# A linear-attention and gated-MLP kernel: key-value state in eight full steps, first loads over two queues, the value splits reordered, the last block halved

## The chip, the cores and the metric

The kernel runs on one core of a Trainium2 chip. Its time is the device time of one execution in microseconds (us); lower is better. A core has five engines with a queue of instructions each: TensorE (PE, with weight loads shown apart as PEld), VectorE (DVE), ScalarE (ACT), GpSimd (POOL) and SyncE (SP), which here only issues DMAs. ScalarE can issue DMAs too. All DMAs are carried out by the core's 16 DMA engines. SBUF is the core's working memory of 128 partitions, PSUM the memory of eight banks into which TensorE writes.

## The reference

The input `x` is 2048 tokens by 640 features, everything in float32. With 32 heads of 20 features each:

```python
xn = _layernorm(x)
qkv = (xn @ wqkv)                          # 640 x 1920
pq, pk = q @ w_phi, k @ w_phi              # per head, 20 x 20
phi_q = concat([softmax(pq), softmax(-pq)])  # 40 features a head
phi_k = concat([softmax(pk), softmax(-pk)])
kv = einsum("bhsf,bhsd->bhfd", phi_k, v)   # per head 40 x 20, summed over tokens
z = phi_k.sum(over tokens)                 # per head 40
o = (phi_q @ kv) / (phi_q @ z + 1e-6)
s = o @ wo
g = silu(gelu(xn @ w1 + b1) @ w2 + b2)     # 640 -> 1536 -> 640
return x + s * g
```

## The kernel before

Tokens are handled in 16 tiles of 128. Every float32 matrix is kept as a high half (a copy rounded to a shorter mantissa) and a low half (what is missing), and a product is three matmuls: high by high, high by low, low by high. A "split" makes these halves: ScalarE copies the high one, and GpSimd or VectorE subtracts it from the original.

The kernel has three phases.

*First phase.* At the start, ten matmuls of constants run on TensorE while the first data arrive. The key projection and the head map `w_phi` are folded into one matrix: `fold_w` multiplies each of five chunks of the transposed key weights (`folds`, loaded from `wqk`) by a block-diagonal matrix `foldb`, which VectorE builds from `w_phi` (`foldc`) and the mask `hmask`; GpSimd makes the mask. The product lies in one of three PSUM banks of kind A, ScalarE takes its high half, VectorE its low half (L183), and then the bank is free. Token tiles are normalised (`norm_a`: statistics, `norm_b` or `norm_act`: scaling), transposed on TensorE (`transpose_x`) and split (`plain`). Then each tile is projected to keys (`project` with `wk`), to values (`value` with `wv`) and later to queries; `feat1` and `feat2` make the exponentials of the feature map, `key_fin` scales them. After every two tiles, `kv_pair` adds them to the key-value state in one PSUM bank, `kvp[0]`: per tile and head one matmul (`kv_acc`) of 32 value columns (20 values, a one, which yields `z`, and columns that belong to the next head) against the head's 40 features. A head's product takes 32 partitions (`32*e`, e from 0 to 3) and 40 columns (`40*s`).

*Second phase.* Twelve units (two token halves by six groups of the hidden layer) compute the MLP: `part` for the first matrix, `down` for the second. Beside it, query features come back from memory, are normalised with `z` (`q_norm`, which needs `z` repeated over all partitions, `zrep`), transposed and written out as `phi_t`. The state is copied out of PSUM in `kv_rest`, its row of `z` is sent to memory and back by `kv_norm` in unit 0, and `kv_state` transposes it and lays it out as the block-diagonal `bdk` and `bdl` in unit 6.

*Third phase.* `num` multiplies `phi_t` by `bdk`; `finish` multiplies by `wo`, by the gate, adds `x` and stores the block of 128 output features by 512 tokens. There are 20 such blocks; the very last one (`end`) is computed in two parts of its columns, each with its own PSUM bank, product, sum and store.

The order on the engines is written by hand in three ways. At the startup all engines run in the order of the code. In the rest of the first phase TensorE and SyncE do, and a scheduler places the work of the others. From the second phase on all engines again run in the order of the code. SyncE issues nearly all loads and stores, in order; a DMA waits until the eighth one before it has landed, since there are eight completion semaphores.

## Time and profile before

| | |
|---|---|
| median of 3 runs | 659.72 us (659.64 to 659.89) |
| profiled execution | 659.86 us, of which the profiled span is 658.1 us |
| TensorE busy | 652.6 us, 99% of the span |
| VectorE, ScalarE, GpSimd busy | 72%, 35%, 58% |
| granted TensorE clock | 0.999 of full speed |
| TensorE waits for other engines behind 1 us | four groups of at most 0.8 us each |
| moved by DMA | 126.97 MB, 193 GB/s on average |

Times in a timeline row are in us from the start of the span; the row gives the start, the time from the first start to the last end, the engine, the line of the kernel, the operation, the tile written and the tiles read, and the number of instructions merged into the row. In square brackets stands the idle time before it and what ended it. A matmul's end is modelled, so that rows of TensorE overlap a little. A row of the chain of waits gives start, length and what the end of the execution then depended on.

### The profile page before, as it was taken

What the parts mean: (1) busy time and instruction counts of PE and PEld (TensorE: products, weight loads), DVE (VectorE), ACT (ScalarE), POOL (GpSimd) and SP (SyncE); (2) the same over time, 40 slices, a digit from 0 to 9 for tenths busy, and PEclk for the clock granted to TensorE, in tenths of its full rate; (3) what the DMA queues carried; (4) which work ended last, traced back from release to release, by engine and by line L of the source; (5) the groups of instructions that cost most, each with busy time, mean ns of one, the idle gap of its engine ahead of it and who ended that gap; (6) DMA issues with size and microseconds to landing.
All of it is one profiled execution on the core that took longest, in us unless ns stands there. A gap on an engine that the chain in (4) does not pass through costs nothing.

```text
span 658.1 us, 11381 instructions
## 1 busy us (share of the span) xinstructions
PE 652.6 (99%) x4437; PEld 568.0 (86%) x4437; DVE 474.1 (72%) x721; ACT 228.3 (35%) x321; POOL 383.7 (58%) x352
## 2 busy tenths in 40 slices
PE   9999999999999999999999999999999999999998
PEld 8999999999999998888888888888888886766867
DVE  5886755888777556768978968759789899853232
ACT  3523313332332227352452454751232424032130
POOL 3655354859577456957778776364462967343321
PEclk9999999999999999999999999999999999999999
DMA  8805162825271226537899799695769499999952
GB/s 319 305 2 148 31 156 86 252 82 157 45 209 66 102 82 231 169 109 251 227 258 316 181 416 333 91 344 218 149 219 234 98 271 205 309 218 253 308 189 81
DMA packets 159678, 126.97 MB, mean 193 GB/s; under 512 B 88976, under 2 KB 127120, under 8 KB 158728
## 3 DMA queue, kind: packets, MB, share of 16 engines
q1 hardware_dynamic: 157320, 115.76, 60.9%
q10 hardware_dynamic: 2304, 10.49, 4.2%
q8 instruction: 35, 0.57, 0.3%
q14 instruction: 19, 0.16, 0.1%
HBM read 81.12 MB, written 45.10 MB: 192 GB/s over the span
## 4 chain that ended last, share of the span: by engine, by line
PE 94%; DMA 3%; DVE 1%; POOL 1%; SPq 0%; issue 0%; DVEq 0%; POOLq 0%
PE pA L331 30%; PE pB L687 24%; PE pB L658 22%; PE pB L842 11%; PE pB L789 2%; PE kv L402 2%; PE pA L172 1%; DMA raw<-in_wv_dram 1%; DMA folds<-in_wqk_dram 1%; DMA xt<-in_x_dram 1%; PE pB L796 1%; POOL wv L147 0%; DMA phi_t<-eq 0%; DVE y L696 0%; POOL e L352 0%
## 5 line engine op out<-in xcount | busy, mean ns | idle before, releaser
L687 PE MATMUL pB<-hs,w2s 128*128 128x512 f32 x720 | 165.7, 389 | 0.0
L687 PEld LDWEIGHTS pB<-hs,w2s 128*128 128x128 f32 x720 | 135.0, 188 | 28.8 <-DVE y L696 0.8
L658 PE MATMUL pB<-xp,w1s 128*128 128x512 f32 x324 | 81.3, 389 | 0.0
L658 PE MATMUL pB<-xd,w1s 128*128 128x512 f32 x324 | 79.3, 389 | 0.0
L357 ACT ACTIVATE e<-e 128x1280 f32<-128x1280 f32 x32 | 40.7, 1273 | 95.5 <-POOL e L352 95.1
L842 PE MATMUL pB<-oT,wo 128*128 128x512 f32 (+2 forms) x315 | 73.0, 383 | 0.0
L658 PEld LDWEIGHTS pB<-xd,w1s 128*128 128x128 f32 x324 | 60.8, 188 | 12.6
L658 PEld LDWEIGHTS pB<-xp,w1s 128*128 128x128 f32 x324 | 60.8, 188 | 12.6
L370 POOL TENSOR_TENSOR eq<-eq,rc 128x1280 f32<-128x1280 f32 x16 | 37.9, 2371 | 56.3 <-DVE rc L746 38.3
L842 PEld LDWEIGHTS pB<-oT,wo 128*128 128x128 f32 x315 | 57.8, 188 | 13.8 <-PE pB L789 2.5
L370 POOL TENSOR_TENSOR e<-e,rc 128x1280 f32<-128x1280 f32 x16 | 39.0, 2441 | 46.4 <-DVE rc L390 46.1
L696 DVE TENSOR_TENSOR y<-pB,y 128x512 f32<-128x512 f32 x100 | 63.2, 676 | 1.4 <-PE pB L687 1.4
L352 POOL TENSOR_TENSOR e<-nr,e 128x640 f32<-128x640 f32 x32 | 44.4, 1388 | 29.2 <-DVE nr L351 24.2
L331 PE MATMUL pA<-wv,xp 128*128 128x320 f32 x384 | 60.0, 310 | 0.3 <-POOL wv L147 0.3
L331 PE MATMUL pA<-wk,xp 128*128 128x320 f32 x384 | 59.7, 310 | 0.0
L663 ACT ACTIVATE pB<-pB,b1t 128x512 f32<-128x512 f32 x48 | 31.8, 662 | 78.7 <-DVE pB L925 28.9
L331 PE MATMUL pA<-wq,xp 128*128 128x320 f32 x384 | 58.8, 309 | 0.0
L331 PEld LDWEIGHTS pA<-wv,xp 128*128 128x128 f32 x384 | 57.0, 188 | 0.5 <-POOL wv L147 0.5
L331 PEld LDWEIGHTS pA<-wk,xp 128*128 128x128 f32 x384 | 56.9, 188 | 0.1
L331 PEld LDWEIGHTS pA<-wq,xp 128*128 128x128 f32 x384 | 56.9, 188 | 0.0
L733 POOL TENSOR_TENSOR ez<-eq,zrep 128x1280 f32<-128x1280 f32 x16 | 47.4, 2960 | 0.9 <-DMA eq<-e_dram 0.9
L430 POOL TENSOR_TENSOR w1s<-raw,w1s 128x640 fp32r<-128x640 f32 (+1 forms) x18 | 27.2, 1513 | 31.4 <-ACT w1s L429 31.3
(138 smaller groups left out, 998.0 us busy)
## 6 DMA issues: line engine op xcount, KB each, us to landing
raw<-in_w_dram SPq DMA_DIRECT2D x42, 320.0 KB, 4.9
e_dram<-e ACTq DMA_DIRECT2D x16, 640.0 KB, 3.6
eq<-e_dram SPq DMA_DIRECT2D x16, 640.0 KB, 5.8
phi_t<-eq SPq DMA_DIRECT2D x64, 160.0 KB, 3.3
phT<-phi_t SPq DMA_DIRECT2D x20, 480.0 KB, 9.5
xt<-in_x_dram SPq DMA_DIRECT2D x16, 320.0 KB, 5.3
xres<-in_xt_dram SPq DMA_DIRECT2D x20, 256.0 KB, 8.5
out_dram<-xres SPq DMA_DIRECT2D x18, 256.0 KB, 5.8
```

Of the source, the lines that this page charges most:

```text
L331: nc.tensor.matmul(ps[:, hf, :HALF], stat_x(q, o, k, a), ws[k][:, b, hf * HALF:(hf + 1) * HALF], start=n == 0, stop=n == 3 * KC - 1)
L352: nc.gpsimd.tensor_tensor(e5[:, :, :, 1, :], nr[:, :, :, None].to_broadcast([P, 2, 16, DH]), e5[:, :, :, 0, :], op=OP.subtract)
L357: nc.scalar.activation(ef, ef, AF.Exp)
L370: nc.gpsimd.tensor_tensor(e3, e3, rc[:, :, None].to_broadcast([P, 64, DH]), op=OP.mult)
L402: nc.tensor.matmul(ps[32 * e:32 * e + 32, 40 * s:40 * s + 40], v[:, 21 * h:21 * h + 32], phi[:, 40 * h:40 * h + 40], start=t == 0 and s == ...
L430: nc.gpsimd.tensor_tensor(sl[:, 1, :n], src, sl[:, 0, :n].bitcast(F32), op=OP.subtract)
L658: nc.tensor.matmul(bank[ch][:], tl[:, a, off + wo_:off + wo_ + P], mov(blk, b), start=new and n == 0, stop=n == len(mms) - 1, skip_group_c ...
L663: nc.scalar.activation(ps, ps, AF.Gelu_apprx_tanh, bias=b1t[:, f:f + 1])
L687: nc.tensor.matmul(ps[:], ws[i][:, b, d * P:(d + 1) * P], hs[o][i][:, a, :], start=i == n == 0, stop=(i, n) == (GF - 1, 2), skip_group_che ...
L696: nc.vector.tensor_tensor(y, ps[:], y, op=OP.add)
L733: nc.gpsimd.tensor_tensor(zv, ef, zf, op=OP.mult)
L842: nc.tensor.matmul(ps[:, mv], w, o[:, mv], start=n == 0, stop=n == 15, skip_group_check=True)
```

## The change

Five things are changed together.

1. `kv_acc` places the heads anew. Six steps of four heads stay as they are; the last eight heads, which took three steps of three, three and two, take two steps of four. The state's columns go from 360 to 320. `kv_rest` copies the state to SBUF without the fills, with columns 240 to 320 twice; `kv_state` makes four transposes instead of three and five products for `bdk` instead of one; `kv_norm` sends eight small rows instead of five.
2. The first loads: of the five chunks of key weights, the first and the fourth go out on ScalarE's queue, and token tile 0 between them; the others stay with SyncE.
3. At the startup, `norm_a(0)` comes ahead of the first fold and `norm_b(0)` behind it, and `split_v(1)` comes ahead of `norm_act(2)`.
4. The head mask is made by two GpSimd instructions over six columns instead of twelve over one, and ahead of the identity.
5. The last block's parts are 256 and 256 columns instead of 384 and 128.

```diff
+    nc.gpsimd.memset(hmask, 1.0)
+    nc.gpsimd.affine_select(out=hmask, in_=hmask, pattern=[[-DH, 6]], compare_op=OP.is_ge, fill=0.0, base=0,
+                            channel_multiplier=1)
+    nc.gpsimd.affine_select(out=hmask, in_=hmask, pattern=[[DH, 6]], compare_op=OP.is_ge, fill=0.0, base=DH - 1,
+                            channel_multiplier=-1)
     ident = const.tile([P, P], F32, name="ident")
...
-    for k in range(6):
-        nc.gpsimd.affine_select(out=hmask[:, k:k + 1], in_=hmask[:, k:k + 1], pattern=[[0, 1]],
-                                compare_op=OP.is_ge, fill=0.0, base=-DH * k, channel_multiplier=1)
...
-    def load_fold(which, mid=None):
+    def load_fold(which, engs):
         tl = folds[:, which]
-        for c in range(KC):
-            nc.sync.dma_start(tl[:, c], wqk[which, c, :, :6 * P].rearrange("p (i t) -> p i t", i=6))
-            if c == 1 and mid is not None:
-                mid()
+        for c, eng in enumerate(engs):
+            if c == 1 and which:
+                x_in(0, nc.scalar)
+            eng.dma_start(tl[:, c], wqk[which, c, :, :6 * P].rearrange("p (i t) -> p i t", i=6))
...
     def kv_acc(t, phi, v):
         ps = kvp[0]
-        for g in range(3):
-            for r in range(3):
-                for e in range(4):
-                    h = 3 * (4 * g + e) + r
-                    if 4 * g + e < NFT and h < H:
-                        s = 3 * g + r
-                        nc.tensor.matmul(ps[32 * e:32 * e + 32, 40 * s:40 * s + 40], v[:, 21 * h:21 * h + 32],
-                                         phi[:, 40 * h:40 * h + 40], start=t == 0 and s == 0, stop=t == NT - 1,
-                                         skip_group_check=True)
+        for s in range(8):
+            for e in range(4):
+                h = 3 * (4 * (s // 3) + e) + s % 3 if s < 6 else 24 + 2 * e + s - 6
+                nc.tensor.matmul(ps[32 * e:32 * e + 32, 40 * s:40 * s + 40], v[:, 21 * h:21 * h + 32],
+                                 phi[:, 40 * h:40 * h + 40], start=t == 0 and s == 0, stop=t == NT - 1,
+                                 skip_group_check=True)
...
-    wkT = load_fold(1, lambda: x_in(0))
+    wkT = load_fold(1, (nc.scalar, nc.sync, nc.sync, nc.scalar, nc.sync))
...
+    norm_a(0)
     fold_w(wkT, range(1), "wk", wk_s)
-    norm_a(0)
-    fold_w(wkT, range(1, 2), "wk", wk_s)
     norm_b(0)
-    fold_w(wkT, range(2, 4), "wk", wk_s)
+    fold_w(wkT, range(1, 4), "wk", wk_s)
...
+    split_v(1)
     norm_act(2)
-    split_v(1)
     split_v(2)
...
-        kvr = const.tile([P, 360], F32, name="kvr")
-        nc.gpsimd.memset(kvr[64:96, 320:360], 0.0)
-        nc.gpsimd.memset(kvr[96:, 240:360], 0.0)
-        for p, a, b in ((P, 0, 240), (96, 240, 320), (64, 320, 360)):
-            nc.scalar.activation(kvr[:p, a:b], kvp[0][:p, a:b], AF.Copy)
+        kvr = const.tile([P, 424], F32, name="kvr")
+        nc.scalar.activation(kvr[:, :320], kvp[0][:, :320], AF.Copy)
+        nc.scalar.activation(kvr[:, 320:400], kvp[0][:, 240:320], AF.Copy)
...
-        for g, m in enumerate((P, P, 96)):
-            nc.tensor.transpose(ps[:120, g * P:g * P + m], kvr[:m, 120 * g:120 * g + 120], ident[:m, :m])
...
+        for i, o in enumerate((0, 120, 240, 280)):
+            nc.tensor.transpose(ps[:120, i * P:(i + 1) * P], kvr[:, o:o + 120], ident[:])
+
+        def heads_of(f, n, blk, h, m):
+            src = ps[:120, 32 * blk:32 * (blk + n)].rearrange("p (f r) -> p f r", r=32)
+            nc.vector.tensor_tensor(bdk[:120, f:f + n, 20 * h:20 * (h + m)].rearrange("p f (h d) -> p f h d", d=20),
+                                    src[:, :, None, :20].to_broadcast([120, n, m, 20]),
+                                    mask[:120, None, h:h + m, None].to_broadcast([120, n, m, 20]), op=OP.mult)
+
+        heads_of(0, 8, 0, 0, 3)
+        heads_of(8, 1, 8, 0, 2)
+        heads_of(8, 1, 9, 2, 1)
+        heads_of(9, 1, 13, 0, 1)
+        heads_of(9, 1, 14, 1, 2)
...
-        for e, m in enumerate((3, 3, 2, 2)):
-            nc.sync.dma_start(zv[e:e + 1, :m], kvr[32 * e + 20:32 * e + 21, :120 * m].rearrange("p (g r) -> p g r", r=120))
-        nc.sync.dma_start(z_dram[1200:2 * D].unsqueeze(0), kvr[84:85, 240:320])
+        for e in range(4):
+            one = kvr[32 * e + 20:32 * e + 21]
+            nc.sync.dma_start(zv[e:e + 1], one[:, :240].rearrange("p (g r) -> p g r", r=120))
+            nc.sync.dma_start(zl[e:e + 1], one[:, 240:320])
...
-        parts = (slice(0, 384), slice(384, 512)) if end else (slice(0, W2), slice(W2, 512))
+        parts = (slice(0, W2), slice(W2, 512))
```

The orders on the engines below are those of the built kernels; a number behind a name tells one buffer from another. First VectorE at the startup, before; `wk0` to `wk2` are the folded key weights, whose low halves these products are, and `xt_153` is token tile 0.

```order
L489 TENSOR_TENSOR folds_74<-folds_74 120x6x120
L183 TENSOR_TENSOR wk0_197<-pA_190,wk0_197 128x640
L196 BN_STATS st_200<-xt_153 128x6 x2
L197 BN_AGGR st_200<-st_200 128x2
L198 TENSOR_SCALAR st_200<-st_200 128x1
L183 TENSOR_TENSOR wk1_213<-pA_206,wk1_213 128x640
L212 TENSOR_SCALAR xt_153<-xt_153,st_200 128x640
L183 TENSOR_TENSOR wk2_224<-pA_217,wk2_224 128x640
```

The same place in the changed kernel, where token tile 0 is `xt_142`:

```order
L482 TENSOR_TENSOR folds_74<-folds_74 120x6x120
L195 BN_STATS st_180<-xt_142 128x6 x2
L196 BN_AGGR st_180<-st_180 128x2
L197 TENSOR_SCALAR st_180<-st_180 128x1
L182 TENSOR_TENSOR wk0_193<-pA_186,wk0_193 128x640
L211 TENSOR_SCALAR xt_142<-xt_142,st_180 128x640
L182 TENSOR_TENSOR wk1_204<-pA_197,wk1_204 128x640
L182 TENSOR_TENSOR wk2_214<-pA_207,wk2_214 128x640
```

The statistics of tile 0 have moved ahead of the first low half, and its normalising ahead of the second.

ScalarE at the startup, before: the normalising of tiles 1 and 2 (`xt_158`, `xt_160`), the high halves of the value weights (`wv`, from `raw`) and of token tile 1 (`b12`, `xp`).

```order
L218 ACTIVATE xt_158<-xt_158,st_245 128x640 [waits DMAHW7_49,DVE_49]
L145 ACTIVATE wv_269<-raw_162 128x640 [waits DMAHW1_49]
L251 ACTIVATE b12_304<-pA_298 128x2x128 [waits PE_49]
L251 ACTIVATE xp_73<-pA_298 128x3x128
L218 ACTIVATE xt_160<-xt_160,st_263 128x640 [waits DMAHW0_49,DVE_49]
L145 ACTIVATE wv_317<-raw_164 128x640 [waits DMAHW2_49]
L145 ACTIVATE wv_320<-raw_166 128x640 [waits DMAHW3_49]
```

The same engine now, from its second instruction on and, behind the line of dots, at the same place as above (tiles 1 and 2 are `xt_148` and `xt_150`):

```order
L163 DMA folds_74<-in_wqk_dram 128x768
L139 DMA xt_142<-in_x_dram 128x640
L163 DMA folds_74<-in_wqk_dram 128x768
L181 ACT_TABLE_LOAD
...
L144 ACTIVATE wv_259<-raw_152 128x640 [waits DMAHW1_49]
L250 ACTIVATE b12_294<-pA_288 128x2x128 [waits PE_49]
L250 ACTIVATE xp_73<-pA_288 128x3x128
L144 ACTIVATE wv_305<-raw_154 128x640 [waits DMAHW2_49]
L217 ACTIVATE xt_150<-xt_150,st_253 128x640 [waits DMAHW0_49,DVE_49]
L144 ACTIVATE wv_310<-raw_156 128x640 [waits DMAHW3_49]
```

Three DMAs now stand ahead of the load of the activation table, and the second value split ahead of the normalising of tile 2.

TensorE at the end of the kernel, before, and behind the line of dots now; a block is 15 matmuls with `wo` and one with the last heads' part `wol`:

```order
L842 MATMUL pB<-oT,wo 128x384 x15
L842 MATMUL pB<-oTl,wol 128x384
L842 MATMUL pB<-oT,wo 128x128 x15
L842 MATMUL pB<-oTl,wol 128x128
...
L843 MATMUL pB<-oT,wo 128x256 x15
L843 MATMUL pB<-oTl,wol 128x256
L843 MATMUL pB<-oT,wo 128x256 x15
L843 MATMUL pB<-oTl,wol 128x256
```

The number of instructions is the same; their columns are 256 in both parts.

More of the change, by code (lines that the diff above doesn't have):

```diff
@@ L135, in hedgehog_gated_mlp_kernel, with load_x @@
     bdl = const.tile([P, 120], F32, name="bdl")
-    def load_x(t):
+    def load_x(t, eng=None):
         xt = row([P, D], F32, "xt")
-        nc.sync.dma_start(xt[:], x[_tok(t) * P:(_tok(t) + 1) * P, :])
+        (eng or nc.sync).dma_start(xt[:], x[_tok(t) * P:(_tok(t) + 1) * P, :])
         return xt
@@ L456, in load_w2, with x_in @@
         return [load_split(w2[f * P:(f + 1) * P, :], "w2s", None, lo) for f in range(g * GF, (g + 1) * GF)]
-    def x_in(t):
-        xts[t] = load_x(t)
-    def fold_loads(which, mid=None):
-        return load_fold(which, mid)
+    def x_in(t, eng=None):
+        xts[t] = load_x(t, eng)
     phase1 = ExitStack()
@@ L478, in hedgehog_gated_mlp_kernel @@
         x_in(t)
-    wqT = load_fold(0)
+    wqT = load_fold(0, (nc.sync,) * KC)
     x_in(6)
@@ L632, in kv_norm @@
     def kv_norm(kvr):
[L633 to L636 removed]
+        zv = z_dram[:960].rearrange("(g e r) -> e g r", e=4, r=120)
+        zl = z_dram[960:2 * D].rearrange("(e r) -> e r", e=4)
+        for e in range(4):
+            one = kvr[32 * e + 20:32 * e + 21]
+            nc.sync.dma_start(zv[e:e + 1], one[:, :240].rearrange("p (g r) -> p g r", r=120))
+            nc.sync.dma_start(zl[e:e + 1], one[:, 240:320])
```

10 lines of the change are left out of this document (1 added, 9 removed).

## The prediction

> **What bounds the kernel now.** I read the page first, then TensorE's waits, then the timeline of the places that the diff touches.
>
> ```profile
> PE 652.6 (99%) x4437; PEld 568.0 (86%) x4437; DVE 474.1 (72%) x721; ACT 228.3 (35%) x321; POOL 383.7 (58%) x352
> PE 94%; DMA 3%; DVE 1%; POOL 1%; SPq 0%; issue 0%; DVEq 0%; POOLq 0%
> ```
>
> TensorE is busy nearly always, and 94% of the chain that ended last is its own work. Of its waits for others behind the warm-up, all below a microsecond, two lie in the first 28 us:
>
> ```profile
> PE pA L172 <- DMA folds<-in_wqk_dram: 0.8, 1, 0.8
> ...
> PE pA L331 <- POOL wv L147: 0.3, 1, 0.3
> ```
>
> So a saving on any other engine is worth a fraction of a microsecond at most. What pays is TensorE time taken away, or the first 28 us, where TensorE still waits for its inputs. The profiled execution took 659.86 us around a span of 658.1, against a median of 659.72: 0.14 is to be taken off at the end. The measurement can tell about 0.2%, or 1.3 us, from no change.
>
> **The change: the key-value state in eight full steps.** Each of the 16 token tiles accumulates 32 heads by matmuls of 32 output columns, side by side on four column groups. Before, a tile took nine steps of 4,4,4,4,4,4,3,3,2 heads; now it takes eight of 4. The number of matmuls stays at 32 a tile. The first rows are the last of eight pairs of tiles on TensorE and the projection behind it; the others count the matmul records of that pair that began by the end of each stretch (us from the span's start).
>
> ```profile
> 241.79 1.48 PE L402 MATMUL kv<-e,v 128*32 128x40 f32 x128
> ...
> 243.20 2.03 PE L331 MATMUL pA<-wq,b 128*128 128x320 f32 x12
> ```
> ```profile
> 241.75:241.88 0.12, 0.09 (x8) 1.00 0.00 0
> 241.75:242.13 0.38, 0.34 (x36) 1.00 0.00 0
> ...
> 241.75:242.88 1.13, 1.09 (x111) 1.00 0.00 0
> ```
>
> A pair has 64 matmuls but 128 records, two a matmul. Among the full steps, from 241.88 to 242.13, 28 records start in 0.25 us: 9 ns each, so a step of four matmuls (8 records) takes 72 ns. At that pace 121 would have begun by 242.88, 1.09 us after the first; there are 111, so steps of three and two heads pass fewer matmuls in the same time. 18 steps of 72 ns make 1.30 us and leave 0.11 for running in and out of the 1.41 from 241.79 to 243.20. So I read the pace as per step, whatever it holds. Sixteen steps make 1.15 + 0.11 = 1.26. Eight pairs save 8 x 0.144 = **1.15 us**, on an engine that doesn't wait between 28 and 550 us; so it reaches the end. Its bounds are nothing, if the pace were by the number, and 1.15.
>
> **First loads over two queues, and the new order behind them.** The scalar engine's queue now issues the first weight chunk, token tile 0 and the fourth chunk; the sync queue has the rest. The rows are from the timeline and, the one of DMA xt, from the chain.
>
> ```profile
> 0.84 4.36 PE L469 MATMUL pA<-const-float32-1.0 128*128 128x128 f32 x20 [0.84 <-PEq L1090]
> 1.26 0.90 SPq L162 DMA_DIRECT2D folds<-in_wqk_dram  x2
> ...
> 7.31 0.82 DVE L183 TENSOR_TENSOR wk<-pA,wk 128x640 fp32r<-128x640 f32 x1 [2.60 <-ACT wk L182]
> 8.05 0.88 DVE L196 BATCH_NORM_STATS2 st<-xt 128x6 f32<-128x320 f32 x2
> ...
> 8.67 2.91 PE L172 MATMUL pA<-folds 120*128 120x120 f32 x24 [0.79 <-DMA folds<-in_wqk_dram]
> ...
> 9.28 0.81 DVE L183 TENSOR_TENSOR wk<-pA,wk 128x640 fp32r<-128x640 f32 x1
> 10.04 0.61 DVE L212 TENSOR_SCALAR xt<-xt,st 128x640 f32<-128x640 f32 x1
> 11.01 0.82 DVE L183 TENSOR_TENSOR wk<-pA,wk 128x640 fp32r<-128x640 f32 x1 [0.35 <-ACT wk L182]
> 11.96 1.53 PE L172 MATMUL pA<-folds 120*128 120x120 f32 x12
> ...
> 13.32 3.83 PE L331 MATMUL pA<-wk,xp 128*128 128x320 f32 x24
> ```
> ```profile
> 2.20 5.39 DMA xt<-in_x_dram
> ```
>
> Token tile 0 lands at 7.59 and the third chunk at about 8.6, where the third fold stops waiting. The fifth fold at 11.96 takes over the PSUM bank of the third, which DVE gives up at 11.83; the first projection follows at 13.32. The four mask instructions that now come first on GpSimd make the fold's right-hand side ready earlier; that is worth nothing, since TensorE's warm-up takes it to 5.2 anyway.
>
> How much earlier the loads land is unknown. Lower end: not at all. Then DVE, which now takes the statistics of tile 0 ahead of the first low half (3 instructions, 8.05 to 9.28, so 1.23), runs from 7.6: statistics to 8.9, low half 9.7, normalising 10.3, second low half 11.1, third 11.9. The fifth fold would start at 12.0: nothing won. Upper end: each load by its earlier issue. An issue takes 0.45 (two in 0.90), so tile 0, second on its queue, goes out at about 1.25 instead of 2.20, and the third chunk, third on the other queue, at 1.7 instead of 2.65; landing 0.95 earlier, tile 0 comes at 6.65. The first high half is there at 7.3 and the statistics end at 7.9; third low half 11.0, projection 12.4: 0.9 won. Between them the DMA engines' own slack decides:
>
> ```profile
> 5.00:6.00 1.00, 1.00 (x11) 1.00 (x11) 0.00 (x0) 0.00 (x0) 0.20 (x2) 1.00 0.70 221
> ...
> 9.00:10.00 1.00, 1.00 (x12) 1.00 (x11) 0.97 (x3) 0.00 (x0) 0.56 (x1) 1.00 1.03 410
> ```
>
> From 5 to 6 us they were 70% busy (the column before the last); by 9 they are full. What earlier issue can fill is some 0.3 us, nearest to the lower end; I take **0.3** earlier. The sync queue's later loads move up by three issues, with none of them waited for in time. The activation table load moves behind three issues of 0.45, from 0.8 to 2.2, and ScalarE's first work comes after 6.5: nothing.
>
> **Value splits.** The second split moves ahead of the normalising of tile 2 on ScalarE.
>
> ```profile
> 19.67 0.92 ACT L218 ACTIVATE xt<-xt,st 128x640 f32<-128x640 f32 x1 [1.08 <-DVE st L217]
> ...
> 21.30 3.11 POOL L147 TENSOR_TENSOR wv<-raw,wv 128x640 fp32r<-128x640 f32 x2 [1.82 <-DMA folds<-in_wqk_dram]
> ...
> 23.56 3.98 PE L331 MATMUL pA<-wv,xp 128*128 128x320 f32 x26
> ...
> 26.18 1.57 POOL L147 TENSOR_TENSOR wv<-raw,wv 128x640 fp32r<-128x640 f32 x1
> ...
> 27.81 0.85 PE L331 MATMUL pA<-wv,xp 128*128 128x320 f32 x4 [0.27 <-POOL wv L147]
> ```
> ```profile
> 31.84 8.80 PE pA L331 x60
> ```
>
> The last row is from the chain: 147 ns a projection matmul of 320 columns. The high half of split 1 (0.7, as the ScalarE copies of that size) fits into the 1.08 in which ScalarE sat idle before 19.67. GpSimd then starts its low half at 19.5 instead of 21.30; split 2 follows at 21.3 and the last, still behind the exponent's differences, ends near 26.5 instead of 27.75. TensorE needed it at 27.4 (26 matmuls of 147 ns after 23.56) and got on at 27.81: **0.4** saved, or nothing if the loads make the rest late.
>
> **Last block in halves.** Rows of TensorE, of DVE behind it, and of the output stores.
>
> ```profile
> 650.23 2.79 PE L842 MATMUL pB<-oT,wo 128*128 128x384 f32 x15
> ...
> 653.03 1.79 PE L842 MATMUL pB<-oT,wo 128*128 128x128 f32 x15
> ...
> 654.66 0.28 PE L842 MATMUL pB<-oTl,wol 120*128 120x128 f32 x1
> ```
> ```profile
> 651.35 0.42 DVE L844 TENSOR_TENSOR y<-pB,y 128x256 f32<-128x256 f32 x1
> ...
> 654.97 0.29 DVE L844 TENSOR_TENSOR y<-pB,y 128x128 f32<-128x128 f32 x1 [0.52 <-PE pB L842]
> ```
> ```profile
> out_dram<-xres SPq DMA_DIRECT2D x2, 128.0 KB, 1.9
> ```
>
> Sixteen matmuls of 384 columns take 2.80, 175 ns each; those of 128 columns 109 each (15 from 653.03 to 654.66), twice what their columns would take on the same line, so a floor. 256 columns aren't in the trace: the straight line from 320 (147) through 384 gives 120, the mean between 109 and 175 gives 142. I take 120, since the floor lies below it. The last one then starts at 650.23 + 31 x 0.12 = 653.95 instead of 654.66: 0.7 saved. DVE's two instructions at the end take 0.42 for 0.29, +0.3; the store carries 64 KB more, +0.2 at the 410 GB/s seen above. That nets 0.2; I take **0.1**, since 256 columns may lie a little above the line. With 142 it is 0.5 lost.
>
> **The state's use.** One transpose more on TensorE (three cost 0.24, from 420.46 to 420.70): **0.1** lost.
>
> ```profile
> 420.46 0.47 PE L623 MATMUL pB<-ident,kvr 128*120 128x128 f32 x3
> 420.70 1.64 PE L687 MATMUL pB<-hs,w2s 128*128 128x512 f32 x6
> ```
> ```profile
> 424.03 0.39 DVE L629 TENSOR_TENSOR bdl<-pB,mask 80x40 f32<-80x40 f32 x3
> ...
> 427.82 0.69 DVE L694 COPY y<-pB 128x512 f32<-128x512 f32 x1 [0.67 <-PE pB L687]
> ```
> ```profile
> 249.01 2.78 SPq L635 DMA_DIRECT2D z_dram<-kvr  x4
> ...
> 274.33 2.96 POOL L733 TENSOR_TENSOR ez<-eq,zrep 128x1280 f32<-128x1280 f32 x1
> ```
>
> DVE gets four small products more, 0.13 each like the three here; its idle 0.67 soon after covers them, and if it didn't, the copies out of PSUM would be late. The sync queue sends eight rows of the normaliser instead of five, 0.7 each, so the replicated copy and the loads behind it go out about 2 us later, with 18 us before their first reader. ScalarE copies the state in two pieces instead of three, and GpSimd loses two fills; neither is waited for.
>
> Sum: -1.15 - 0.3 - 0.4 - 0.1 + 0.1 = -1.85. The profiled 659.86 becomes 658.0, the median 657.9.
>
> **Rivals.** *Loads land as before.* The DMA share of 1.0 at 9 us speaks for it, the 0.70 against. Then the 0.3 is gone: 658.2. [...]
>
> *The two queues alternate finely.* Then the second chunk lands with tile 0 and the third with the fourth, at 7.6 and about 9.5 (384 KB a chunk, 0.95 at 410 GB/s): the third fold starts 0.9 later and so does the projection. Sum -0.65 (-1.85 + 0.3 + 0.9): 659.1, no measurable change. Nothing in the trace of before has two queues at once.
>
> *The state is paced by its matmuls.* Then 1.15 is gone: 659.0. The cumulative counts speak against it. [...]
>
> *Slower: tile 0 is late.* DVE now stands before its first low half until tile 0 has landed, and every low half, fold and projection queue behind it. Up to 7.6 this costs nothing; from there each microsecond delays the first projection by one. The other terms save 1.5, so it decides from 9.2, and measurably from 10.5. If the sync queue's chunks are served first, tile 0 lands like the fifth chunk, at about 10.5 (8.6 plus two of 0.95): 2.9 later, 661.1. Its place second on a queue of its own speaks against it.
>
> **How the numbers follow.** Forecast 0.48; loads as before 0.18; fine alternation 0.14; paced by number 0.10; tile 0 late 0.10. The forecast's own range is 657.2 to 658.4, by 0 to 0.9 at the start and 0.5 at the tail. The range 657.0 to 659.3 takes in the next three and leaves out the late tile and the tails. Faster by over 0.2% means under 658.4: most of the first two cases, 0.63. Same: the rest of these, the third and fourth, 0.27. Slower 0.10.
>
> **What would show it.** From the start of a state pair to the next projection: 1.26, not 1.41. The first projection at about 13.0. TensorE waits for no value split. Last matmuls at 0.12 each, the last store out 0.3 earlier than at 655.6. Wrong would be: a pair of 1.41, a first fold or statistics that wait for tile 0 beyond 8 us, or a new wait on TensorE between 250 and 275 or after 424 us.

## The result, and the profile after

The changed kernel takes 658.55 us (median of 13 runs, 658.04 to 658.90) against 659.89 (13 runs, 659.49 to 660.50): a ratio of 0.9978, with a 95% interval of 0.9970 to 0.9987. That is 1.3 us faster (0.9 to 2.0). The forecast was 1.85 faster, 657.9, with a range of 657.0 to 659.3. The profiled execution took 658.55 with a span of 656.8, so 1.31 less than the one of before.

First the busy times of the page after, and what is left of TensorE's waits:

```profile
PE 651.7 (99%) x4438; PEld 567.1 (86%) x4438; DVE 472.9 (72%) x725; ACT 228.5 (35%) x320; POOL 381.3 (58%) x340
```
```profile
PE pA L462 <- PEq L1091: 0.8, 1, 0.8
PE pB L797 <- DVE y L697: 0.4, 1, 0.4
```

The waits for the third weight chunk (0.8) and for the value split (0.3) are gone; the bound is the same. Now the timeline of the kernel after, at the places to which the prediction gave a term (start, us, engine, line, operation):

```profile
5.24 6.05 PE L171 MATMUL pA<-folds 120*128 120x120 f32 x48
6.00 0.89 DVE L195 BATCH_NORM_STATS2 st<-xt 128x6 f32<-128x320 f32 x2 [1.35 <-DMA xt<-in_x_dram]
...
13.03 1.20 PE L330 MATMUL pA<-wk,xp 128*128 128x320 f32 x6
...
23.29 4.56 PE L330 MATMUL pA<-wv,xp 128*128 128x320 f32 x30
24.47 1.57 POOL L146 TENSOR_TENSOR wv<-raw,wv 128x640 fp32r<-128x640 f32 x1
27.68 1.92 PE L330 MATMUL pA<-wv,b 128*128 128x320 f32 x12
...
240.26 1.37 PE L398 MATMUL kv<-e,v 128*32 128x40 f32 x128
241.57 2.02 PE L330 MATMUL pA<-wq,b 128*128 128x320 f32 x12
...
419.01 0.60 PE L613 MATMUL pB<-ident,kvr 128*120 128x128 f32 x4
419.36 3.02 PE L688 MATMUL pB<-hs,w2s 128*128 128x512 f32 x12
...
648.92 1.97 PE L843 MATMUL pB<-oT,wo 128*128 128x256 f32 x15
...
652.65 0.28 PE L843 MATMUL pB<-oTl,wol 120*128 120x256 f32 x1
652.96 0.42 DVE L845 TENSOR_TENSOR y<-pB,y 128x256 f32<-128x256 f32 x1 [0.96 <-PE pB L843]
```

Going by the starts of the same matmuls in the two traces, the kernel after is 0.29 us ahead at the first projection (13.03 for 13.32) and 0.81 ahead at the second value projection (27.68 for 28.49), so the split gave 0.52. From the first matmul of a pair to the next projection it took 1.41 in all eight pairs before; now it takes 1.30 in two of them (the last, from 240.26 on, is one) and 1.32 in the six others, which makes 0.77. With what the projections just behind the pairs gain, the lead grows by 0.83, to 1.64 at 246 us. From there it shrinks: 0.19 in the first feed-forward unit, 0.13 from the transposes on; 1.31 are left at 648.92, against 650.23. In the last block matmuls of 256 columns follow each other at 0.12 and the last one starts 2.0 earlier than before. From the block's start to the landing of the last store (655.78 by its semaphore, 657.25 before) it takes 6.86 instead of 7.02, so 0.16 are won; the closing behind the landing takes 0.17 longer and eats it.

That longer closing is no accident of one execution. From the last landing to the end of the span it takes 0.90 in all four profiles of kernels with the old state, and 1.06 to 1.09 in all ten with the new one. Behind its wait for the last store SyncE still checks one other semaphore in the former and four in the latter, 0.06 each. The state's eight rows instead of five make three transfers more in all (346 for 343), and the last store then has another semaphore, whose turn in these checks comes earlier.

The place in the first feed-forward unit was not in the prediction. Before and after, on DVE, GpSimd and TensorE:

```profile
252.74 2.64 DVE L147 TENSOR_TENSOR w2s<-raw,w2s 128x640 fp32r<-128x640 f32 x2 [2.44 <-ACT w2s L145]
252.93 1.76 POOL L352 TENSOR_TENSOR e<-nr,e 128x640 f32<-128x640 f32 x1
254.66 1.32 POOL L418 TENSOR_TENSOR st<-raw 128x256 f32<-128x256 f32 x1
256.06 0.74 POOL L418 TENSOR_TENSOR st<-st,raw 128x256 f32<-128x256 f32 x1
257.94 2.20 PE L658 MATMUL pB<-xp,w1s 128*128 128x512 f32 x9
```
```profile
250.88 1.27 POOL L351 TENSOR_TENSOR e<-nr,e 128x640 f32<-128x640 f32 x1
251.16 2.94 DVE L146 TENSOR_TENSOR w2s<-raw,w2s 128x640 fp32r<-128x640 f32 x2 [2.44 <-ACT w2s L144]
252.11 1.32 POOL L414 TENSOR_TENSOR st<-raw 128x256 f32<-128x256 f32 x1
253.51 1.20 POOL L414 TENSOR_TENSOR st<-st,raw 128x256 f32<-128x256 f32 x1
256.35 2.33 PE L659 MATMUL pB<-xp,w1s 128*128 128x512 f32 x9
```

Without the two fills GpSimd begins its exponent differences (`e`) before DVE begins to split two weight tiles, and not behind. In the trace, whichever of the two begins second is the slower one: before, DVE's first split takes 0.83 and GpSimd's differences 1.76; now the differences take 1.27 and DVE's first split 1.67. The second split takes 1.90 before and 1.36 now, so the two splits together take 2.94 instead of 2.64. TensorE's nine matmuls behind take 2.33 instead of 2.20; with 0.06 just ahead of them, that is the 0.19.

### The profile page after: what moved, and what is told of

It is laid out like the page before. It is cut to its first block, busy times and chain, and to the rows that moved or that the text cites. A ratio compares the mean times of both kernels' runs of the same rounds, so it can differ in the third digit from the quotient of the medians.

```text
span 656.8 us, 11378 instructions
## 1 busy us (share of the span) xinstructions
PE 651.7 (99%) x4438; PEld 567.1 (86%) x4438; DVE 472.9 (72%) x725; ACT 228.5 (35%) x320; POOL 381.3 (58%) x340
## 4 chain that ended last, share of the span: by engine, by line
PE 98%; DVE 1%; DMA 0%; SPq 0%; issue 0%; DVEq 0%
PE pA L330 32%; PE pB L688 24%; PE pB L659 22%; PE pB L843 11%; PE pA L171 2%; PE pB L790 2%; PE kv L398 2%; PE pA L462 1%; PE pB L797 1%; PE pA L316 1%; DVE y L697 0%; DMA phi_t<-eq 0%; DVE wolh L767 0%; DVE dn L364 0%; SPq L756 0%; DVE wol L768 0%
## 5 line engine op out<-in xcount | busy, mean ns | idle before, releaser
L843 PE MATMUL pB<-oT,wo 128*128 128x512 f32 (+1 forms) x315 | 72.3, 381 | 0.0
L659 PEld LDWEIGHTS pB<-xp,w1s 128*128 128x128 f32 x324 | 60.7, 188 | 12.8 <-DVE pB L926 0.3
```

What stands on the lines that cost most here:

```text
L659: nc.tensor.matmul(bank[ch][:], tl[:, a, off + wo_:off + wo_ + P], mov(blk, b), start=new and n == 0, stop=n == len(mms) - 1, skip_group_c ...
L843: nc.tensor.matmul(ps[:, mv], w, o[:, mv], start=n == 0, stop=n == 15, skip_group_check=True)
```

## The experiments

Times are compared with runs of the kernel before on the same chip. A few tenths can't be told from the medians, so terms are read from the traces and the medians are given beside them.

**Each part alone.** The state alone:

```diff
-        for g in range(3):
-            for r in range(3):
...
+        for s in range(8):
+            for e in range(4):
+                h = 3 * (4 * (s // 3) + e) + s % 3 if s < 6 else 24 + 2 * e + s - 6
...
-        kvr = const.tile([P, 360], F32, name="kvr")
+        kvr = const.tile([P, 424], F32, name="kvr")
```

> The kernel before with the key-value state in eight full steps, and with the state's copy, transposes, products and normaliser rows that belong to it; nothing else. Theory S (the prediction's): a state pair is paced by its steps alone, 72 ns each, so the pair goes from 1.41 to 1.26 us and the kernel loses 1.15 us, less 0.1 for the fourth transpose: about 1.05. Theory P (read from the kernel after, where the pair took 1.30 to 1.32): a step of two or three heads cost about half a full one, so the pair goes to 1.30 to 1.32, eight pairs give 0.8 and, with the transpose, some 0.7 remains. Theory N (paced by the number of matmuls): nothing, the pair stays at 1.41. The small stall of TensorE in the first feed-forward unit of the kernel after (0.15 to 0.2) comes here too if it stems from the state's new order, and stays away if it stems from the earlier start of that unit by more than this edit gives.

Measured: 659.82 against 659.91, ratio 1.0002 (0.9993 to 1.0011): nothing. The same kernel once more, to see whether that holds:

> The kernel with the state alone once more, without any other edit, for a second profile and more times: its first ones were 0.1 us faster than the kernel before, where the pairs alone save 0.7 to 0.8. Theory T: the wait near 139 us goes with the round trip near 78 us; a trip below 4.3 leaves TensorE without a wait there and the end 0.4 earlier than the kernel before, a trip of 4.6 or more brings the wait back. Rival (the wait belongs to this edit whatever the trip): the wait is there at any trip.

Measured: 659.86 against 659.74, ratio 1.0002 (0.9993 to 1.0011). The pairs do take 1.30 to 1.32 in both profiles (one of them 1.36), as theory P has it, but the gain is given back. In the second profile TensorE's lead over the kernel before grows by 0.42 in the four pairs up to 131 us, loses 0.65 at a value projection near 139, gains 0.42 in the other four pairs, loses 0.21 in the first feed-forward unit and 0.15 from the transposes on. The closing, 0.16 longer, takes more. The place near 139, and one on ScalarE ahead of it, of this kernel:

```profile
105.07 0.33 ACTq L384 DMA_DIRECT2D e_dram<-e  x1
105.81 0.74 ACT L251 ACTIVATE xp<-xr 128x640 fp32r<-128x640 f32 x1 [0.77 <-ACT e L357]
...
139.60 0.18 DVE L351 TENSOR_TENSOR nr<-mn,mx 128x32 f32<-128x32 f32 x1
139.82 1.99 PE L331 MATMUL pA<-wv,b 128*128 128x320 f32 x12 [0.42 <-DVE nr L351]
```

and of the kernel before:

```profile
105.06 0.33 ACTq L384 DMA_DIRECT2D e_dram<-e  x1
105.49 0.74 ACT L251 ACTIVATE xp<-xr 128x640 fp32r<-128x640 f32 x1 [0.46 <-ACT e L357]
...
139.25 0.18 DVE L351 TENSOR_TENSOR nr<-mn,mx 128x32 f32<-128x32 f32 x1
140.06 1.19 PE L331 MATMUL pA<-wv,b 128*128 128x320 f32 x7
```

TensorE starts 0.22 behind DVE's difference `nr` when it waits for it, and 0.81 behind when it doesn't, so the kernel before had a margin of 0.6 there. And ScalarE starts its copy 0.41 after the DMA issue ahead of it instead of 0.10, in all profiles with the state alone and in none of the others, the kernel after among them. What holds it there isn't settled. So undoing the other parts wasn't a clean cut: it added a stall of its own.

The loads alone, and the value splits alone:

```diff
-    wkT = load_fold(1, lambda: x_in(0))
+    wkT = load_fold(1, (nc.scalar, nc.sync, nc.sync, nc.scalar, nc.sync))
```

> The kernel before with the first loads over two queues, the mask first and the statistics of tile 0 ahead of the first low half; state, value splits and last block as before. In the kernel after, TensorE's matmuls of the warm-up and the first folds changed from 213 to 112 ns apart at 6.35 us; in the kernel before at 4.81. Theory C (what the loads give is decided by the moment of that change): the folds follow each other without a wait from 5.2, and the first projection starts near 12.4 if the change comes at 4.8, near 13.0 if it comes at 6.35, half a microsecond per microsecond of delay while folds are running. Theory L (the prediction's: the loads land only 0.3 earlier): 13.0 whatever the moment of the change, with a wait for a load left in the folds.

```diff
-    norm_act(2)
     split_v(1)
+    norm_act(2)
```

> The kernel before with the second value split moved ahead of the normalising of tile 2; nothing else. The prediction's theory: TensorE's wait of 0.27 us for the fourth value split disappears and the second value projection starts 0.4 earlier than 28.49, so about 28.1, and the end comes 0.4 earlier. Rival: the wait in the kernel before was set by the splits behind the second one (their weights or GpSimd's exponent differences), and the wait stays or only half of it goes: 28.3 to 28.5.

The loads give 659.52, ratio 0.9995 (0.9987 to 1.0004); the splits 659.38, ratio 0.9992 (0.9983 to 1.0001), both against 659.91. With the loads alone the first projection starts at 12.80 and no fold waits, and the wait for the split is still there. That is nearer to theory C (the change from 213 to 112 ns comes at 5.9 here) than to theory L, since no fold waits for a load. With the splits alone the wait for the split is gone:

```profile
5.24 5.82 PE L171 MATMUL pA<-folds 120*128 120x120 f32 x48
...
12.80 3.84 PE L330 MATMUL pA<-wk,xp 128*128 128x320 f32 x24
...
27.29 0.85 PE L330 MATMUL pA<-wv,xp 128*128 128x320 f32 x4 [0.27 <-POOL wv L146]
```
```profile
23.24 4.56 PE L331 MATMUL pA<-wv,xp 128*128 128x320 f32 x30
27.64 1.92 PE L331 MATMUL pA<-wv,b 128*128 128x320 f32 x12
```

From the first value matmul to the next projection it took 4.93 before (23.56 to 28.49), and takes 4.40 now, so 0.53. The prediction's theory holds, its 0.4 counted the wait and not the gap of 0.1 that restarting costs.

The last block in halves alone:

```diff
-        parts = (slice(0, 384), slice(384, 512)) if end else (slice(0, W2), slice(W2, 512))
+        parts = (slice(0, W2), slice(W2, 512))
```

> The kernel before with the last block in two halves of 256 columns instead of 384 and 128; nothing else. The prediction's theory: the last matmul starts 0.7 earlier, DVE's last two instructions and the bigger last store give back 0.6, so 0.1 is won. Rival, read from the kernel after: the store takes 0.28 and DVE 0.26 longer and the rest is lost in the last wait, so nothing is won or lost: within 0.1 of the kernel before from the start of the last block (650.23) to the last landing (657.25), which is 7.02 us there.

Measured: 659.71 against 659.91, ratio 0.9997 (0.9989 to 1.0006). In the trace, from the block's start (649.97) to the last landing (656.84) 6.87 instead of 7.02: 0.15, near the 0.1 of the prediction, and the rival that nothing is won falls. The medians of the four parts alone add up to 1.0 to 1.2 us (0.1 or -0.1, 0.4, 0.5, 0.2); the whole gives 1.3.

**What a step costs.**

```diff
-        for s in range(8):
+        for s in range(9):
...
-                h = 3 * (4 * (s // 3) + e) + s % 3 if s < 6 else 24 + 2 * e + s - 6
+                h = 3 * (4 * (s // 3) + e) + s % 3 if s < 6 else 24 + 2 * e + (s - 6) % 2
```

> The kernel after with a ninth step of four heads added to the state; the step repeats heads of the seventh, its sums land in columns that nothing reads, so this kernel does work that isn't needed. The pair took 1.30 to 1.32 us after and 1.41 before. Theory S (the prediction's: every step costs 72 ns whatever it holds, and 0.11 is for running in and out): nine steps are nine steps, the pair takes 1.41 again and the time is that of the kernel before less the other parts. Theory F (a full step is 72 ns, running in and out is 0.15, so the three short steps before cost 0.066 each, nearly but not quite a full one: 1.41 less 12 full steps of 0.072 and less 0.15, divided by 6): the pair takes 1.45 to 1.47. Theory N (by the number of matmuls): 1.30 x 72 / 64 = 1.47 as well, but N would have left the pair at 1.41 in the kernel after, which it did not.

Measured: 659.30 against 659.88, 0.75 slower than the kernel after. From the chain of waits, the last pair with nine full steps, and with eight (after):

```profile
241.04 1.45 PE kv L398 x142
```
```profile
240.33 1.30 PE kv L398 x126
```

One full step more in each tile costs about 0.145 a pair (1.448 to 1.468 for 1.303 to 1.323, and one pair of 1.481): 72 ns a step, theory F. Nine steps with three short ones took 1.41; theory S, under which they would be the same, falls. Theory N, by the number of matmuls, gives the same 1.47 here; it falls because the same 64 matmuls went from 1.41 to 1.30. A short step cost 0.066 in the mean, which is what is left of 1.41 when the 12 full steps take 72 ns each and running in and out 0.15; so theory P's half of a full step falls too. Eight pairs at 0.145 make 1.16, but the medians differ by 0.75: in the profile the first projection starts at 12.58 here, 0.45 earlier than in the kernel after, and that hides the rest.

**The second queue.**

```diff
-    wkT = load_fold(1, (nc.scalar, nc.sync, nc.sync, nc.scalar, nc.sync))
+    wkT = load_fold(1, (nc.sync,) * KC)
...
-                x_in(0, nc.scalar)
+                x_in(0)
```

> The kernel after with all first loads on the sync queue, tile 0 again behind the second chunk; mask, statistics and the rest as after. Theory Q (the second queue is what brings the loads earlier): the landings go back to about those of before (tile 0 7.6, third chunk 8.5), the statistics wait until 7.6 and hold back the first low half, TensorE waits for the folds again, and the first projection starts at 13.3 or a little later. Theory M (the mask first and the order of DVE do it, or the loads come earlier by chance): 13.0 or earlier, with tile 0 near 6.0. The moment at which the spacing of the matmuls goes from 213 to 112 ns is to be taken off: up to 0.4 us of start for a change at 4.2 instead of 6.35, as far as the folds are running by then.

Measured: 658.79 against 659.88, 0.24 slower than the kernel after by medians. Timeline:

```profile
7.34 0.89 DVE L195 BATCH_NORM_STATS2 st<-xt 128x6 f32<-128x320 f32 x2 [3.46 <-DMA xt<-in_x_dram]
8.84 2.91 PE L171 MATMUL pA<-folds 120*128 120x120 f32 x24 [1.12 <-DMA folds<-in_wqk_dram]
13.49 2.81 PE L330 MATMUL pA<-wk,xp 128*128 128x320 f32 x17
```

Tile 0 is back at 7.3, the third fold waits 1.1, the projection starts at 13.49. Theory Q: the second queue is what brings the loads (with tile 0's place in it, which this edit moves too). What it does to the rate, from the stretches of before and of after (the last two columns are the share of the DMA engines and GB/s):

```profile
3.00:4.00 1.00, 1.00 (x7) 1.00 (x7) 0.20 (x1) 0.00 (x0) 1.00 (x9) 1.00 1.08 353
4.00:5.00 1.00, 1.00 (x7) 1.00 (x7) 0.70 (x1) 0.00 (x0) 1.00 (x3) 1.00 1.03 287
```
```profile
3.00:4.00 1.00, 1.00 (x7) 1.00 (x7) 0.26 (x1) 0.49 (x1) 0.13 (x1) 1.00 1.04 412
4.00:5.00 1.00, 1.00 (x6) 1.00 (x6) 0.65 (x1) 0.00 (x0) 0.00 (x0) 1.00 1.04 402
5.00:6.00 1.00, 1.00 (x7) 1.00 (x6) 0.01 (x1) 0.00 (x0) 0.00 (x0) 1.00 1.05 415
```

From 3 to 6 us it moves 412, 402 and 415 GB/s where one queue moved 353, 287 and 221 in the kernel before, and 341, 362 and 281 in this run. The second queue brings more than the time of issuing: tile 0 is issued 0.94 earlier with two queues than in this run (1.25 for 2.19), but lands 1.35 earlier (5.97 for 7.32). Why one queue moves less isn't settled. Its issues, 0.45 each, come faster than the chunks land (0.95 apart from 7.6 to 10.4 us in the kernel before), and the DMA engines of the kernel before were counted 30% idle only from 5 to 6 us; from 3 to 5 they were counted full (1.08 and 1.03 in the rows above) while they moved less.

**The warm-up.**

```diff
-        for i in range(5):
+        for i in range(4):
             nc.tensor.matmul(pw[:, 0, :P], one, one, start=True, stop=True)
```

> The kernel after with eight instead of ten warm-up matmuls on constants. In the kernel after the folds follow the warm-up without a wait, from 5.24, and the right-hand side of the folds is ready at 4.65. Theory W (TensorE's own work sets the start now): the folds start at about 4.7 and the first projection up to half a microsecond earlier than 13.03; exactly 0.85 less work at 213 ns or 0.44 at 112 ns, cut by a wait for the right-hand side or the first chunk. Rival (fewer matmuls ahead make the change from 213 to 112 ns come later, and the folds pay for it): the change comes after 6.35, and the first projection starts at 13.0 or later.

Measured: 658.35 (658.07 to 658.51) against 659.88; against the 658.55 of the kernel after no difference that can be told. Timeline:

```profile
4.88 2.94 PE L171 MATMUL pA<-folds 120*128 120x120 f32 x24 [0.48 <-DVE folds L482]
8.36 2.91 PE L171 MATMUL pA<-folds 120*128 120x120 f32 x24 [0.55 <-DMA folds<-in_wqk_dram]
13.02 3.25 PE L330 MATMUL pA<-wk,xp 128*128 128x320 f32 x20
```

The folds start 0.4 earlier, wait 0.55 for the third chunk, and the projection starts where it did. Neither theory quite holds: the change from 213 to 112 ns came early (4.1), against the rival, but the time saved at the front was lost to a load that came at 8.3 in this execution.

Over all profiles, the start goes by two things. One is the moment at which TensorE's matmuls go from 213 to 112 ns apart; the trace's record of the granted clock begins at that moment (the table of stretches shows 1.00 all through), at 4.8 us in the kernel before, at 6.35 in the kernel after, and at 4.1 to 6.5 over all profiles. With two queues and no wait of a fold for a load of over 0.12 us the first projection starts at 12.58 for a moment of 5.0, at 12.64 for 5.5, at 12.80 for 5.9 and at 13.03 for 6.35; in two profiles a fold came 0.2 to 0.3 late, and it starts at 12.60 for 4.6 and at 12.95 for 5.5. What sets that moment, which lies 2.4 us apart in the earliest and the latest profile, isn't shown. The other is the queues: these six profiles with two queues have a mean of 12.8, six with one queue as before start the projection at 12.99 to 13.61 (mean 13.2). So the edits at the start are worth 0.4 in the mean; the two single profiles of before and after happened to show 0.29.

**The unit with the two fills.**

```diff
-        kvr = const.tile([P, 424], F32, name="kvr")
+        kvr = const.tile([P, 584], F32, name="kvr")
+        nc.gpsimd.memset(kvr[64:96, 424:464], 0.0)
+        nc.gpsimd.memset(kvr[96:, 464:584], 0.0)
```

> The kernel after with two fills on GpSimd put back, of the size of those that the change removed and at their old place (they write columns that nothing reads, so they are work that isn't needed). In the first feed-forward unit the kernel after and the one with the state alone gave back 0.15 us of TensorE time, the kernels with the loads, the splits or the halves alone did not. Theory G (the two fills of 0.12 and 0.19 us held GpSimd's exponent differences back until DVE's split of two weight tiles was nearly over; without them GpSimd's work lies beside that split, which takes 2.94 instead of 2.64, and the exchange of DVE against GpSimd makes TensorE wait): the split takes 2.64 again, TensorE waits for no copy there, and 0.15 us come back although GpSimd does more. Rival (the wait comes from the eight normaliser rows on the sync queue, or from the shorter copies on ScalarE): the split stays at about 2.9 and the wait stays.

```profile
250.75 2.64 DVE L146 TENSOR_TENSOR w2s<-raw,w2s 128x640 fp32r<-128x640 f32 x2 [2.44 <-ACT w2s L144]
255.87 2.20 PE L661 MATMUL pB<-xp,w1s 128*128 128x512 f32 x9
```

Theory G: the split takes 2.64 again, the nine matmuls 2.20, and TensorE's lead over the kernel after grows by 0.19 at this place. The median is 658.44, no difference that can be told from 658.55, and three of the ten runs took 659.8 to 660.9, where the kernel after never took more than 658.9. So the 0.19 is shown in the trace alone; that the whole kernel gains by the fills is not shown. The same on the kernel with the state alone:

> The kernel before with the state in eight full steps and the two fills on GpSimd left in at their old place (into columns that nothing reads). With the state alone the gain of 0.7 to 0.8 us in the pairs was given back at three places: 0.40 at the value projection near 139 us, 0.16 in the first feed-forward unit, 0.14 at the four transposes. Theory G: the 0.16 does not come. Theory T: what is given back near 139 depends on how long the statistics' round trip near 78 us happens to take in this execution: nothing below 4.3, up to 0.4 at 4.7. Then the end lies 0.2 to 0.6 before the kernel before. Rival (the state's steps save nothing at the end, whatever the execution): the same time as the kernel before, with TensorE waiting at the same two places.

Measured: 659.48 against 659.74 by medians, 0.38 below the state alone; but three of the eleven runs took 661.3 to 662.3, so that the ratio is 1.0006 (0.9996 to 1.0017) and nothing is won that can be told. Why kernels with the fills have such long runs isn't known. In the trace nothing is lost in the unit; 0.15 is lost near 139 and 0.10 at the transposes. The gap on ScalarE is 0.41 here too. The round trip's own length (4.66, 4.44 and 4.69 us in the three profiles with the state) doesn't order the losses near 139 (0.42, 0.65, 0.15), so theory T falls in the form in which it was put; TensorE's lead on arriving there does (0.55, 0.82, 0.29), against a difference that comes at 139.60 to 139.64 in all three.

**The place near 139 us.** Times from the traces (us): DVE's statistics of token tile 10, whose load comes behind a round trip of statistics through DRAM; the difference `nr`; the value projection.

| kernel | statistics | `nr` | from one to the other | projection behind `nr` |
|---|---|---|---|---|
| before | 88.93 | 139.25 | 50.32 | 0.81 |
| state alone, first and second | 89.08, 89.04 | 139.64, 139.60 | 50.56, 50.56 | 0.22, 0.22 |
| loads alone | 89.06 | 139.32 | 50.26 | 0.22 |
| splits alone | 88.65 | 138.97 | 50.32 | 0.24 |
| after | 87.79 | 138.01 | 50.22 | 0.82 |
| after, with fills | 87.87 | 138.10 | 50.23 | 0.30 |
| after, eight warm-up matmuls | 88.30 | 138.51 | 50.21 | 0.29 |

Whatever TensorE does, `nr` comes 50.2 to 50.3 behind the statistics (50.6 with the gap on ScalarE): a second bound runs through DVE, GpSimd and ScalarE beside TensorE, and TensorE is 0 to 0.6 behind it. The other profiles up to here fit: 50.2 to 50.3 with the halves alone, one queue or nine steps, 50.5 with the state and the fills, which has the gap on ScalarE. With nine steps TensorE comes 1.15 behind `nr`, and `nr` comes no later for it. To make it later, two small reads that nothing uses went ahead of the broadcast read:

```diff
+            if q == 4:
+                for i in range(2):
+                    idle = const.tile([P, 2], F32, name=f"idle{i}")
+                    nc.sync.dma_start(idle[:], st_dram[q, i])
```

> The kernel after with two small reads of the statistics' DRAM copy put ahead of the broadcast read of the second pair of tiles (near 78 us), on the sync queue; nothing reads what they bring, so they only make that round trip longer. In the profiles so far the round trip there (from the store's issue to the broadcast read's) took 3.92 to 4.67 us, and the time between DVE's last difference of the following pair and the value projection on TensorE near 139 us shrank from 0.82 to about 0.3 as it grew; in the kernel with the state alone, at 4.66, TensorE waited there 0.2 us and started 0.40 later against the kernel before than just ahead of it. Theory T (the round trip sets when DVE is through, and TensorE's saved time is given back there as soon as the trip is longer than about 4.5): with about 0.7 us more in the trip TensorE waits for DVE's difference near 139, and the end comes 0.3 to 0.8 later. Rival (the wait in the kernel with the state alone came from something else, such as its own copies): the start of that projection does not move.

```profile
139.24 1.99 PE L334 MATMUL pA<-wv,b 128*128 128x320 f32 x12 [0.49 <-DVE nr L354]
```
```profile
PE pB L794 <- DMA phT<-phi_t: 4.5, 5, 1.6
```

There, theory T holds: the statistics come 0.9 later than in the kernel after, `nr` 1.0 later (50.3 behind them again), and TensorE waits 0.49 and loses 0.65. But the kernel takes 665.5 (median of 4, 664.25 to 670.3), some ten times the loss expected. In the profiled execution, the longest of the four, TensorE loses most of it behind 320 us: it waits 4.5 us for transfers of `phi` alone, and its granted clock stands at 0.50 from 638 to 643 us. Why two reads near 80 us do that isn't settled, and nothing is drawn from its time. The other way round, with the loads of tiles 10 and 11 issued ahead of the round trip:

```diff
+        if t == 5:
+            x_in(10)
+            x_in(11)
         if t > 3:
             pair_stats(t + 4)
...
-        if t == 5:
-            x_in(10)
```

> The kernel after with the two fills on GpSimd put back (as above) and the loads of token tiles 10 and 11 issued ahead of the statistics' store and broadcast read near 78 us instead of behind them. In all profiles so far the time from DVE's statistics of tile 10 (88 to 89 us) to its last difference ahead of the value projection near 139 us was 50.2 to 50.6 us, whatever TensorE did; TensorE's distance behind that difference was between 0.22 (it waits) and 0.82. Theory C (a chain through DVE, GpSimd and ScalarE, started by that load, runs beside TensorE there and takes back what TensorE has saved before 139 us as soon as the load is late): with the load 4 us earlier the statistics come about 2 us earlier at least, until the broadcast read itself is the last thing waited for; the distance grows to over 1 us, TensorE doesn't wait, and the time is that of the kernel with the fills, 658.4, less up to 0.3 in the mean over executions. Rival (the chain is started by something else, such as the broadcast read): statistics earlier, but the distance stays at 0.3 to 0.8 and the time stays.

```profile
84.08 0.88 DVE L195 BATCH_NORM_STATS2 st<-xt 128x6 f32<-128x320 f32 x2
...
135.65 0.18 DVE L350 TENSOR_TENSOR nr<-mn,mx 128x32 f32<-128x32 f32 x1
...
138.74 1.92 PE L330 MATMUL pA<-wv,b 128*128 128x320 f32 x12
```

The statistics come 3.7 earlier than in the kernel after, `nr` 2.4 earlier, and the projection stands 3.1 behind it instead of 0.3 to 0.8. Theory C, as to the chain: that load starts it, but only as far as 2.4 of the 3.7 us. From the statistics to `nr` it now takes 51.6, so something else has become the later one, and what it is isn't shown. The time is 658.26 against 659.99, ratio 0.9979 (0.9970 to 0.9988): the lowest median of all, but 0.2 to 0.3 below the kernel after or the one with the fills can't be told from none.

## Why the prediction was right, and where not

The direction, the range and the bound were right: TensorE's own time sets the end, and most of what was taken from it or from its first 28 us arrived. The total is 0.54 short of the forecast: one term was too big, and two costs were put at nothing. Of the terms:

- State, 1.15: the mechanism was right, the size not. The step that failed is "so I read the pace as per step, whatever it holds", with 0.11 left for running in and out. A full step does take 72 ns, but a step of three or two heads took 66 in the mean, and running in and out 0.15: 0.83 in all with the projections behind. The rival "paced by its matmuls" fell with the pair of 1.30.
- "On an engine that doesn't wait between 28 and 550 us; so it reaches the end": true in the profile after, but by a margin nobody had looked at. Near 139 us the kernel before had 0.6 to spare, other executions almost nothing, and with the state alone the saving went there.
- "GpSimd loses two fills; neither is waited for": no one waits for the fills, but they made GpSimd begin behind DVE's split and not ahead of it. 0.19 lost, a term that was missing. It is one of the prediction's own signs of being wrong, "a new wait on TensorE between 250 and 275".
- Loads, 0.3: 0.29 in the two profiles, 0.4 in the mean, by another sum, so the number was right by luck. Tile 0 landed near 6.0, beyond the upper end taken (6.65), so "nearest to the lower end" was wrong; in the kernel after the matmuls went from 213 to 112 ns apart late (6.35, against 4.8 before) and that hid it. "Loads land as before" and "tile 0 is late" fell with the landing at 5.97. "Alternate finely" had the sharing right and its cost wrong: the second chunk lands with tile 0 (5.64 and 5.97) and the third near the fourth (7.71 and 8.41), but all of them earlier than that rival's 7.6 and 9.5, since more is moved in all, and no fold waits.
- Value splits, 0.4: 0.52. Last block, 0.1: 0.16 to the last landing. Transposes: 0.13 lost for 0.1. DVE's products: hidden, as said. The eight normaliser rows are hidden where the prediction looked, in the unit, but not at the end: with three transfers more the closing takes 0.17 longer, the other term that was missing. That is read from the fourteen traces; no run changes the number of transfers alone.

The sum of the profiled execution: -0.29 - 0.52 - 0.83 + 0.19 + 0.13 - 0.16 + 0.17 = -1.31, as measured, against -1.85 forecast. Of the difference, 0.32 is the state, 0.19 the fills and 0.17 the closing; the splits and the last block gave 0.18 more than forecast and hid part of it.

## What to carry to other kernels

When the bound engine is at 99%, look for the engine that is second there: measure how far behind its last wait each of its starts is, since here a margin of 0.6 us decided whether a saving reached the end. Before removing an instruction that nobody waits for, see what its engine does in the time that falls free, and beside whom. And price the short case of a repeated step on its own, by one experiment that makes all steps full, rather than from the pace of the full ones.

## What the runs showed that was not expected

A matmul of 32 by 40 in a group of four costs 18 ns (72 a step) and a group of two or three hardly less than one of four (66 in the mean, worked out from the pair of 1.41). Putting back 0.31 us of useless fills on GpSimd brought TensorE 0.19 in one unit: of GpSimd's exponent differences and DVE's split the one that begins second is slower, 1.76 for 1.27 or 1.67 for 0.83. With three small transfers more the closing of the kernel takes 0.17 longer: its last store then has another semaphore, with four checks behind its own and not one. And with two 1 KB reads ahead of one broadcast read the kernel took 665.5, 7 us more; the profiled execution lost most of it behind 320 us, far behind them.
